# Normalising the softmax output: the sums copied to all rows of their head by one selector product, reciprocal and scaling from PSUM

## The chip, the cores and the metric

One core of a Trainium2 chip runs the kernel. It has five engines that work side by side, each with its own queue of instructions: TensorE (PE in the profile; its weight loads are PEld), VectorE (DVE), ScalarE (ACT), GpSimd (POOL) and SyncE (SP), which issues the DMA transfers. On-chip memory is SBUF, with 128 rows called partitions, and PSUM, into which TensorE writes its products; the kernel uses it in tiles of 512 float32 values a partition, called banks below. The metric is the device time of one launch in microseconds (us), as the median of several runs.

## The reference: what is computed

Two independent layers read inputs of length 2048 and width 448, and their outputs stand side by side. The first is a state-space convolution done by Fourier transforms. The second is attention over all keys with 16 heads of width 28, and the change lies there:

```python
scores = jnp.einsum("bhqd,bhkd->bhqk", q, k) * scale
p = _softmax(scores, axis=-1)
o = jnp.einsum("bhqk,bhkd->bhqd", p, v)
return (lambda x, *d: x.transpose(*d))(o, 0, 2, 1, 3).reshape(B, S, D) @ wo
```

The kernel computes exponentials first, multiplies them with the values, and divides the product by the sum of the exponentials at the end. That last division is what is changed.

## The kernel before

Attention is cut into 16 units: G = 4 groups of HG = 4 heads, times NQ = 4 blocks of CQ = 512 queries. Within a unit, NK = 16 steps go over blocks of 128 keys. One main loop of 256 steps runs through all of them. Each head has 32 partitions of a 128-partition tile: 28 value columns, then a column of ones (row DH = 28 of the head's 32), whose product with the exponentials is the softmax sum, and three columns of zeros.

A step issues its work in the order of the list ORDER (line 34): 'm' are products for the row maxima of a later unit (`max_mm`, tile pm), which VectorE reduces (ScalarE first copies the kdif one to tile rl); 's' are score products (`s_mm`, tile pss), which ScalarE turns into exponentials (tile p); 'v' is one of VectorE's power steps for the convolution kernel (tiles g and zg); 'pv' is the value product (`pv_step`, tile po); 'k' is other work on the convolution kernel; 'f' is a slot in which one job of the rest is done. From the main loop on, all engines keep the order in which the program is written (`KEPT["a"]`), so an instruction that waits holds up everything behind it on its engine.

What a slot does is decided in `slot` (line 957): first whatever stands in the list `urgent` and is due, then the output projection, the parts of the convolution kernel, the transform of the input, and the spectrum and finishing jobs. `soon_slot(gap, f)` (line 950) puts f into `urgent`, due `gap` slots later. The gaps are in UG (line 40).

Every max product and every job in a slot takes a PSUM bank from `w_tile` (line 125), and the banks go round in a ring: three in the main loop (pool ps_m, line 562), four once the convolution kernel is complete (pool ps_f, line 1016). A bank can be written again only when its last reader is done.

When a unit's last value product is issued, `fin` (line 734) copies it from PSUM to tile o by ScalarE and puts two parts into slots. `sums` (gap 2): 16 small products with o as the weights and the selector `sel` (128x4) as the moving operand turn the sums into a layout with queries on the partitions; VectorE takes the reciprocal of 16 values a partition (tile r), and ScalarE spreads them over 512 columns (tile rb). `scale` (gap 4): 16 products with the identity turn rb back to heads on the partitions, and VectorE multiplies with o into tile on. A float32 product shows as two records, so these are 32 records each. For the first three groups, on is stored to DRAM (`on_d`) for later; for the last group it goes into the output projection (`project`, with tile og for the stored groups and the weights in tile ua), four products of 128 queries that come due PD = 2 steps after `fin`. `mm32` splits a product into pieces of 32 weight columns that run at once in four column groups of TensorE.

Of the kernel before, what the change touches and what calls it, by code (L numbers as in the profile page):

```python
# [8 lines left out]
F32 = mybir.dt.float32  # L9
F32R = mybir.dt.float32r  # L10
I32 = mybir.dt.int32
AF = mybir.ActivationFunctionType
# [9 lines left out]
DH = 28  # L22
G = 4
HG = H // G
# [12 lines left out]
FX, PD, GAP = 1, 2, 3  # L37
FL = {"s": 2, "f": 3}
S0, SP, SW, SD, PW, E3 = 0, 4, 0, 5, 37, 8
UG = (2, 2, 4)  # L40
PS = 1
SGB, XB, XL = 2, 5, 4
K0, KP, KD, UP = 0, 3.5, 4, 3
# [47 lines left out]
def body(ctx, tc, a, out):  # L91
    nc = Engines(tc)
# [4 lines left out]
    def pool(stack, name, bufs=1, space=None, side=None):  # L97
        kw = {} if space is None else {"space": space}
        if side:
            kw["side"] = side  # L100
        return stack.enter_context(tc.tile_pool(name=name, bufs=bufs, reuse_waits="tile", **kw))
# [13 lines left out]
    const = pool(ctx, "const")  # L115
    ident = const.tile([128, 128], F32, name="ident")
    nc.sync.dma_start(ident, a["ident"])
    sel = const.tile([128, HG], F32, name="sel")
    kones = const.tile([128, 1], F32, name="kones")
    w1 = const.tile([128, 2, 128], F32, name="w1")  # L120

# [3 lines left out]
    def w_tile():  # L125

        n_ring[0] += 1
        return ps_w[0].tile([128, CQ], F32, name=f"pm{n_ring[0] % ps_w[1]}")
# [7 lines left out]
    def mm32(o, w, x_, start, stop, at=0):  # L136

        for i in range(w.shape[-1] // 32):
            c = slice(32 * i, 32 * i + 32)
            nc.tensor.matmul(o[c], w[:, c], x_, start=start, stop=stop, tile_position=(0, at + 32 * i))  # L140
# [53 lines left out]
    def max_join(u):  # L194
        m_u[u, 1] = q_p.tile([128, HG * 4], F32, name="m1", bufs=2)
        nc.vector.tensor_reduce(m_u[u, 1], m_u[u].rearrange("p a b c -> p (a b) c"), axis=AX.X, op=ALU.max)
# [15 lines left out]
    with ExitStack() as st:  # L212
# [47 lines left out]
        t = a["A_log_dt"]  # L260
# [294 lines left out]
    kq_p = pool(kq_st, "kq_p")  # L555
# [178 lines left out]
    def fin(u, s_):  # L734
        g, c = divmod(u, NQ)
        o = kq_p.tile([128, CQ], F32, name="o")
        nc.scalar.activation(o, o_u[u], AF.Copy)
        on = kq_p.tile([128, CQ], F32, name="on", bufs=2)
        rb = kq_p.tile([128, 4, HG, 32], F32, name="rb")
        og = og_u.pop(u, None)  # L740

        def sums():
            pw = w_tile()
            for t in range(4):
                mm32(pw[:, t * HG:(t + 1) * HG], o[:, t * 128:(t + 1) * 128], sel, start=True, stop=True)
            r = kq_p.tile([128, 4, HG], F32, name="r", bufs=2)
            nc.vector.reciprocal(r, pw[:, :4 * HG].rearrange("p (t h) -> p t h", h=HG))
            nc.scalar.activation(rb, r[:, :, :, None].to_broadcast([128, 4, HG, 32]), AF.Copy)

        def scale():  # L750
            pw = w_tile()
            for t in range(4):
                mm32(pw[:, t * 128:(t + 1) * 128], rb[:, t].rearrange("p h e -> p (h e)"), ident, True, True)
            nc.vector.tensor_tensor(on, o, pw, ALU.mult)
            if g < G - 1:
                nc.sync.dma_start(on_d[c][g], on)
            else:
                p_due.extend((s_ + PD + PS * t, lambda t=t: project(t)) for t in range(4))

        def project(t):  # L760
            pw = w_tile()
            ts = slice(t * 128, (t + 1) * 128)
            for g2 in range(G):
                mm32(pw[:, :D], og[:, g2, ts] if g2 < G - 1 else on[:, ts], wo_t[g2 // 2][:, g2 % 2, :],
                     start=g2 == 0, stop=g2 == G - 1)
            y = kq_p.tile([128, D], F32, name="y", bufs=2)
            nc.scalar.activation(y, pw[:, :D], AF.Copy)
            q0 = c * CQ + t * 128
            nc.sync.dma_start(out[q0:q0 + 128, D:], y)

        soon_slot(UG[1], sums)
        soon_slot(UG[2], scale)

    fk = {}

# [174 lines left out]
    def soon_slot(gap, f):  # L950
        n_urgent[0] += 1
        urgent.append((n_slot[0] + gap, n_urgent[0], f))
        q = sorted(urgent)
        urgent.clear()
        urgent.extend(q)
# [38 lines left out]
    def k_next():  # L994

        if last[0] is not None and not powers["e"] and not powers["g"]:
            if last[0] + 3 < NB:
                load_sd(last[0] + 3)
            last[0] = None
# [6 lines left out]
    for s in range(NS):  # L1006
# [26 lines left out]
        for op in ORDER:  # L1033
            if op[0] == "s":
                ps.append(s_mm(u, kt, int(op[1])))
            elif op[0] == "f":
                slot(s)
            elif op[0] == "v":
                vec()
            elif op == "k":  # L1040
                k_next()
                k_begin(s)
                k_seed(s)
                for _ in range(3):
                    if powers["e"]:
                        powers["e"].popleft()()
            elif op == "pv":
                if prev:
                    pv_step(*prev)
                    if prev[1] == NK - 1:  # L1050
                        fin(prev[0], s)
            elif sm < NS:
                max_mm(sm // NK, sm % NK, int(op[1]))
        for _ in range(FX if late[0] else 0):
            slot(s)
        if sm < NS and sm % NK == NK - 1:
# [3 lines left out]
            max_join(sm // NK)  # L1060
            soon_slot(UG[0], end)
        k_next()
        prev = (u, kt, ps)
    pv_step(*prev)
    fin(prev[0], NS)
    s = NS
    while urgent or p_due or m_due or u_due or any(q[k] for q in (f_jobs, f_tasks, f_loaded) for k in "sf"):
# [7 lines left out]
def constants():  # L1075
    import numpy as np
    k = {}
    k["ident"] = np.eye(128)
    sel, ones = np.zeros((128, HG)), np.zeros((128, 1))
    for j in range(HG):  # L1080
        sel[32 * j + DH, j] = 1.0
        ones[32 * j + DH:32 * j + DH + 2] = 1.0
    k["sel"], k["kones"] = sel, ones
    k["pw2"] = np.tile(2.0 ** np.arange(LV), (128, 1))
    n1, k1 = np.arange(N1), np.arange(N1)
    n2, k2 = np.arange(N2), np.arange(N2)
    th = 2 * np.pi * np.outer(n1, k1 + 0.25) / N1
    w1 = np.zeros((2, 128, 128))
    wb = np.zeros((2, 2, N1, 2, N1))
    for j in range(4):  # L1090
        w1[0, 32 * j:32 * j + 32, 32 * j:32 * j + 32] = np.cos(th)
        w1[1, 32 * j:32 * j + 32, 32 * j:32 * j + 32] = np.sin(th)
    for h in range(2):
        wb[h, 0, :, h, :] = np.cos(th).T / L
        wb[h, 1, :, h, :] = np.sin(th).T / L
    k["w1"] = w1.transpose(1, 0, 2)
    k["wb"] = wb.transpose(0, 1, 2, 4, 3).reshape(128, N2)
    ph = 2 * np.pi * ((k1[:, None, None] + 0.25) * n2[None, :, None] / L + n2[None, :, None] * k2[None, None, :] / N2)
    c, s = np.cos(ph).transpose(1, 0, 2), np.sin(ph).transpose(1, 0, 2)
    m2 = np.zeros((2, N2, N1, 2, 64))  # L1100
    m2[0, :, :, 0], m2[0, :, :, 1] = c, s
    m2[1, :, :, 0], m2[1, :, :, 1] = -s, c
    k["m2u"] = m2.reshape(2, 16, 4, N1, 128).transpose(1, 0, 2, 3, 4).reshape(128, N1, 128)
    wa = np.zeros((2, 64, N1, N2, 2))
    ct, st = c.transpose(2, 1, 0), s.transpose(2, 1, 0)
    wa[0, ..., 0], wa[0, ..., 1] = ct, -st
    wa[1, ..., 0], wa[1, ..., 1] = st, ct

    wa = wa.reshape(2, 64, N1, 2, 2, 16, 2).transpose(0, 1, 2, 5, 4, 3, 6)
    k["mw"] = np.concatenate([m2.reshape(128, N1, 128), wa.reshape(128, N1, 128)], -1)  # L1110
    return {n: v.astype(np.float32) for n, v in k.items()}
# [18 lines left out]
```

## Time and profile before

| | |
|---|---|
| median of 3 runs | 1304.37 us (1303.61 to 1306.14) |
| span of the profiled execution | 1301.1 us |
| the runs' median less this span | 3.3 us |
| normalisations in the span | 16; reciprocals from 320.0 to 1279.4 us |
| mean granted TensorE clock | 0.978 of full speed |

The profiled execution is one run of the program, read by the hardware's profiler; its span goes from the first to the last instruction. A row of a group of instructions gives the line, engine, operation, output<-input tiles, the shape, the count, then the busy time in us and the mean length of one in ns, then the idle time of the engine ahead of them with what ended it. All lines read L75, because a helper there records every operation; the tiles tell the operations apart. A row of a timeline gives the start and the length in us. A row of a table by stretches gives the stretch, its length, then busy time and instruction count of PE, PEld, DVE, ACT and POOL, the granted TensorE clock, the share of DMA time and GB/s. The ends of matmuls are modelled and consecutive ones overlap, so distances from start to start tell more than lengths.

### The profile page before, as it was taken

What the parts mean: (1) busy time and instruction counts of PE and PEld (TensorE: products, weight loads), DVE (VectorE), ACT (ScalarE), POOL (GpSimd) and SP (SyncE); (2) the same over time, 40 slices, a digit from 0 to 9 for tenths busy, and PEclk for the clock granted to TensorE, in tenths of its full rate; (3) what the DMA queues carried; (4) which work ended last, traced back from release to release, by engine and by line L of the source; (5) the groups of instructions that cost most, each with busy time, mean ns of one, the idle gap of its engine ahead of it and who ended that gap; (6) DMA issues with size and microseconds to landing.
All of it is one profiled execution on the core that took longest, in us unless ns stands there. A gap on an engine that the chain in (4) does not pass through costs nothing.

```text
span 1301.1 us, 33177 instructions
## 1 busy us (share of the span) xinstructions
PE 1228.2 (94%) x12625; PEld 701.0 (54%) x12625; DVE 948.0 (73%) x2106; ACT 952.4 (73%) x2068; POOL 871.1 (67%) x736
## 2 busy tenths in 40 slices
PE   6878985899999999999999999999999999999997
PEld 5657763355555555555555555555555555544433
DVE  5887896987777887787788888888888655645111
ACT  4775763488888888888888888888887766756552
POOL 3676683298888878888869999998996212424421
PEclk9888997999999999999999999999999999999999
DMA  6677769835866555458644131733425453647656
GB/s 194 203 258 244 249 206 294 237 77 124 195 137 149 124 146 148 140 147 231 181 126 96 54 95 32 182 91 83 103 51 148 153 158 133 201 144 244 198 162 174
DMA packets 200088, 205.35 MB, mean 158 GB/s; under 512 B 95993, under 2 KB 158521, under 8 KB 197881
## 3 DMA queue, kind: packets, MB, share of 16 engines
q1 hardware_dynamic: 199928, 203.23, 56.2%
q8 instruction: 100, 1.64, 0.5%
q14 instruction: 60, 0.48, 0.1%
HBM read 120.73 MB, written 82.18 MB: 156 GB/s over the span
## 4 chain that ended last, share of the span: by engine, by line
PE 71%; DVE 10%; DMA 6%; POOL 5%; ACT 3%; issue 3%; SPq 0%; POOLq 0%; ACTq 0%; DVEq 0%
PE pm L75 40%; PE pss L75 16%; PE po L75 15%; DVE tri L75 2%; DVE mx L75 2%; POOL e L75 1%; POOL qhat L75 1%; DMA k<-hl 1%; ACT tri L75 1%; DVE qhat L75 1%; DVE sg L75 1%; DMA tri<-in_B_wqkv 1%; DVE px L75 1%; DMA khat<-k 1%; DMA ut<-in_A_u 1%
## 5 line engine op out<-in xcount | busy, mean ns | idle before, releaser
L75 ACT ACTIVATE p<-pss 128x512 f32<-128x512 f32 x1024 | 560.9, 609 | 111.6 <-PE pss L75 108.6
L75 PE MATMUL pss<-qhat,khat 128*128 128x512 f32 x1024 | 402.5, 399 | 1.5 <-ACT p L75 1.4
L75 DVE TENSOR_REDUCE mx<-pm 128x1 f32<-128x512 f32 x500 | 321.4, 684 | 109.2 <-PE pm L75 107.1
L75 PE MATMUL pm<-khat,qhat 128*128 128x512 f32 x749 | 326.3, 438 | 3.4 <-DVE mx L75 2.1
L75 POOL TENSOR_TENSOR e<-e,sdb 128x256 f32<-128x256 f32 x168 | 202.0, 1202 | 116.2 <-ACT e L75 61.2
L75 PE MATMUL po<-p,v 128*32 128x512 f32 x2048 | 269.1, 594 | 0.0
L75 POOL TENSOR_TENSOR e<-e,eu 128x256 f32<-128x256 f32 x168 | 248.4, 1478 | 13.2
L75 PEld LDWEIGHTS pm<-khat,qhat 128*128 128x128 f32 x749 | 141.0, 189 | 199.7 <-ACT p L75 47.8
L75 DVE CUSTOM_DVE_ANT_0 rl<-pm,rl 128x512 f32<-128x512 f32 x249 | 171.4, 688 | 65.2 <-ACT rl L75 61.5
L75 PEld LDWEIGHTS pss<-qhat,khat 128*128 128x128 f32 x1024 | 190.2, 188 | 45.7 <-issue 10.8
L75 POOL TENSOR_TENSOR eu<-e,sdb 128x256 f32<-128x256 f32 x168 | 202.2, 1203 | 0.0
L75 POOL TENSOR_TENSOR p<-pr,pr 64x448 f32<-64x448 f32 x64 | 73.3, 1145 | 158.5 <-PE pm L75 133.2
L75 ACT ACTIVATE rl<-pm 128x512 f32<-128x512 f32 x249 | 150.8, 606 | 20.4 <-PE pm L75 20.4
L75 DVE TENSOR_TENSOR g<-g,zg 128x128 f32<-128x128 f32 x392 | 162.1, 413 | 3.4
L75 PE MATMUL pm<-xh,khat 112*128 112x512 f32 x256 | 94.1, 451 | 23.2 <-DVE hl L75 11.1
L75 PE MATMUL pm<-kdif,qhat 128*128 128x512 f32 x249 | 100.5, 404 | 2.6 <-DMA v<-v 1.3
L75 DVE TENSOR_TENSOR zg<-g,zg 128x128 f32<-128x128 f32 x224 | 88.0, 393 | 5.0
L75 PEld LDWEIGHTS pm<-e,g 128*32 128x32 f32 x3584 | 57.2, 109 | 43.8 <-issue 16.1
L75 DVE TENSOR_TENSOR pr<-pm,ub 128x448 f32<-128x448 f32 x64 | 37.0, 619 | 56.4 <-PE pm L75 42.0
L75 PEld LDWEIGHTS pm<-xh,khat 112*128 112x128 f32 x256 | 54.2, 217 | 39.4 <-DVE hl L75 12.9
L75 PE MATMUL pm<-e,g 128*32 128x64 f32 x3584 | 73.0, 222 | 1.9 <-POOL e L75 1.9
L75 ACT ACTIVATE y<-pm 128x448 f32<-128x448 f32 x48 | 26.5, 553 | 58.2 <-PE pm L75 33.8
(134 smaller groups left out, 1470.3 us busy)
## 6 DMA issues: line engine op xcount, KB each, us to landing
sdb<-sd SPq DMA_DIRECT2D x56, 336.0 KB
khat<-k SPq DMA_DIRECT2D x64, 256.0 KB
qhat<-q SPq DMA_DIRECT2D x64, 256.0 KB
sd<-sg SPq DMA_DIRECT2D x8, 1456.0 KB
k<-hl SPq DMA_DIRECT2D x16, 512.0 KB
q<-hl SPq DMA_DIRECT2D x16, 512.0 KB
mw<-in_mw SPq DMA_DIRECT2D x16, 512.0 KB
sd<-qhat SPq DMA_DIRECT2D x8, 896.0 KB
```

The lines of the kernel that those rows point to most:

```text
L75: i = f(*args, **kw)
```

## The change

The selector is now 128x128: column 32j to 32j+31 have their one in the row that holds the sum of head j. One product with this selector as the weights and o as the moving operand puts each head's sum on all 32 partitions of the head, for all 512 queries. VectorE takes the reciprocal of the whole 128x512 block in place in PSUM and multiplies it with o into on. The part `sums`, the tiles r and rb and ScalarE's copy are gone, and `scale` moves into the slot that `sums` had.

```diff
-UG = (2, 2, 4)
+UG = (2, 2)
...
-    sel = const.tile([128, HG], F32, name="sel")
+    sel = const.tile([128, 128], F32, name="sel")
...
         on = kq_p.tile([128, CQ], F32, name="on", bufs=2)
-        rb = kq_p.tile([128, 4, HG, 32], F32, name="rb")
         og = og_u.pop(u, None)
-
-        def sums():
-            pw = w_tile()
-            for t in range(4):
-                mm32(pw[:, t * HG:(t + 1) * HG], o[:, t * 128:(t + 1) * 128], sel, start=True, stop=True)
-            r = kq_p.tile([128, 4, HG], F32, name="r", bufs=2)
-            nc.vector.reciprocal(r, pw[:, :4 * HG].rearrange("p (t h) -> p t h", h=HG))
-            nc.scalar.activation(rb, r[:, :, :, None].to_broadcast([128, 4, HG, 32]), AF.Copy)
 
         def scale():
             pw = w_tile()
-            for t in range(4):
-                mm32(pw[:, t * 128:(t + 1) * 128], rb[:, t].rearrange("p h e -> p (h e)"), ident, True, True)
+            mm32(pw, sel, o, start=True, stop=True)
+            nc.vector.reciprocal(pw, pw)
             nc.vector.tensor_tensor(on, o, pw, ALU.mult)
...
-        soon_slot(UG[1], sums)
-        soon_slot(UG[2], scale)
+        soon_slot(UG[1], scale)
...
-    sel, ones = np.zeros((128, HG)), np.zeros((128, 1))
+    sel, ones = np.zeros((128, 128)), np.zeros((128, 1))
     for j in range(HG):
-        sel[32 * j + DH, j] = 1.0
+        sel[32 * j + DH, 32 * j:32 * j + 32] = 1.0
```

## The prediction

> **What bounds the kernel now.** I read the page first (busy time and the chain that ended last), then the same busy times by stage.
>
> ```profile
> span 1301.1 us, 33177 instructions
> PE 1228.2 (94%) x12625; PEld 701.0 (54%) x12625; DVE 948.0 (73%) x2106; ACT 952.4 (73%) x2068; POOL 871.1 (67%) x736
> ...
> PE 71%; DVE 10%; DMA 6%; POOL 5%; ACT 3%; issue 3%; SPq 0%; POOLq 0%; ACTq 0%; DVEq 0%
> ```
> ```profile
> 300.00:900.00 600.00, 595.93 (x7150) 331.60 (x7142) 489.69 (x1165) 503.27 (x1158) 514.04 (x404) 1.00 0.54 132
> 900.00:1050.00 150.00, 148.82 (x1719) 84.37 (x1715) 120.92 (x279) 118.84 (x259) 105.41 (x83) 1.00 0.41 114
> 1050.00:1200.00 150.00, 149.64 (x1496) 76.77 (x1488) 81.15 (x167) 93.79 (x184) 44.03 (x36) 1.00 0.55 172
> ```
> In the second fence the busy times stand in the order PE, PEld, DVE, ACT, POOL; then comes the granted clock. TensorE sets the end and is never without work from 300 us on. But VectorE is not far behind where most of the change falls: 490 of 600 us and 121 of 150 us, 81% busy. It has little idle time to take up new work before 1050 us and much after it.
>
> **What goes and what comes, by the groups of instructions.** Busy us, then the mean of one in ns:
>
> ```profile
> L75 PE MATMUL pm<-sel,o 128*32 128x4 f32 x512 | 7.0, 175 | 0.3 <-ACT o L75 0.3
> L75 PE MATMUL pm<-ident,rb 128*32 128x128 f32 x512 | 17.3, 275 | 0.7 <-ACT rb L75 0.7
> L75 ACT ACTIVATE rb<-r 128x512 f32<-128x512 f32 x16 | 10.1, 630 | 5.0 <-DVE r L75 5.0
> L75 DVE RECIPROCAL r<-pm 128x16 f32<-128x16 f32 x16 | 4.0, 250 | 0.0
> L75 DVE TENSOR_TENSOR on<-o,pm 128x512 f32<-128x512 f32 x16 | 10.9, 683 | 2.3 <-PE pm L75 2.1
> L75 DVE TENSOR_SCALAR mh<-pm 16x128 fp32r<-16x128 f32 x15 | 4.2, 277 | 5.9 <-PE pm L75 5.5
> L75 DVE TENSOR_SCALAR dt_all<-pt 56x8 f32<-56x8 f32 x5 | 0.5, 150 | 0.3 <-PE pt L75 0.3
> L75 DVE TENSOR_SCALAR px<-px 8x56 f32<-8x56 f32 x5 | 0.9, 177 | 0.1
> ```
> Sixteen times in the run (once per group of heads and block of queries) a unit is normalised. I give each part its price.
>
> *The reciprocal grows from 16 to 512 elements a row; no row shows one of that length.* VectorE's other operations that read PSUM fix the scale: 8 elements take 150 ns and 128 take 277, so (277-150)/120 = 1.06 ns an element and 150-8 = 142 ns beside. A reciprocal of 16 at that rate would take 159 ns; it took 250. The excess of 91 ns is either a fixed cost, or the reciprocal is slower for each element. The lower bound is the first: 250 + 496 x 1.06 = 0.78 us. If the fixed part is 142 ns, an element costs (250-142)/16 = 6.8 ns and 512 take 3.6 us. If the fixed part is the smaller one of the 8x56 row (177-56 x 1.06 = 118 ns), an element costs 8.3 ns and 512 take 4.35 us. The upper bound, no fixed part at all, is 250/16 x 512 = 8.0 us. I take 3.6: it uses the fixed part of operations that, like this one, read PSUM, and a fixed surplus of 91 ns for one opcode has no like among these rows. The Trainium skill says, in "VectorE: DVE Perf Modes", section "First, the fixed hardware budget", that the reciprocal runs as an iterative divide with a repeat count of 8. By it 512 elements would be an estimated 8 x 1.06 x 512 = 4.3 us, close to the 4.35 case; the row alone can't tell 6.8 from 8.3 ns.
>
> That the result goes back to PSUM I cost at nothing: the same power step writes SBUF in 412 ns and PSUM in 425.
>
> ```profile
> L75 DVE TENSOR_TENSOR g<-g,zg 128x256 f32<-128x256 f32 x224 | 92.4, 412 | 1.5
> L75 DVE TENSOR_TENSOR zg<-g,zg 128x256 f32<-128x256 f32 x168 | 71.4, 425 | 3.1
> ```
>
> *TensorE.* Two rounds of 32 records go; one of 8 records of 128x512 comes, the shape of a value product (po). I take one unit, the normalisation at 874 us, as the example, first TensorE, then VectorE (columns: start, length, engine):
>
> ```profile
> 874.16 0.43 PE L75 MATMUL pm<-sel,o 128*32 128x4 f32 x32
> 874.44 1.06 PE L75 MATMUL po<-p,v 128*32 128x512 f32 x8
> 875.43 0.50 PE L75 MATMUL pm<-khat,qhat 128*128 128x512 f32 x1
> ...
> 876.47 0.39 PE L75 MATMUL pm<-kdif,qhat 128*128 128x512 f32 x1
> ...
> 877.71 1.08 PE L75 MATMUL pm<-ident,rb 128*32 128x128 f32 x32
> 878.61 1.04 PE L75 MATMUL po<-p,v 128*32 128x512 f32 x8
> 879.47 0.63 PE L75 MATMUL pm<-e,g 128*32 128x64 f32 x32
> ```
> ```profile
> 875.62 0.25 DVE L75 RECIPROCAL r<-pm 128x16 f32<-128x16 f32 x1
> 875.79 0.38 DVE L75 TENSOR_TENSOR g<-g,zg 128x256 f32<-128x256 f32 x1
> 876.09 1.28 DVE L75 TENSOR_REDUCE mx<-pm 128x1 f32<-128x512 f32 x2
> ```
> From start to next start the sums hold TensorE 0.28 us (874.16 to 874.44) and the spreading product 0.90 (877.71 to 878.61); a product of po's shape 0.86 (878.61 to 879.47). So 1.18 goes and 0.86 comes: 0.3 us gained a unit.
>
> *ScalarE* loses a copy of 0.63 us. It is 84% busy at most (503 of 600) and not the bound: nothing on the path. *SP*: the selector's load grows from 2 to 64 KB, at 16 us, with its first use at 319; the store of the scaled output is now queued two slots earlier, ahead of the next query load, which is needed only a unit (some 57 us) later. The freed slot brings other due work forward but takes none away. All nothing.
>
> *The wait that comes.* In the main loop three PSUM banks go round among max products, jobs and this product, and every engine keeps program order. In the example the selector product takes one bank, the next two max products (the first at 875.43) the others, and the third (the kdif one, 876.47) needs the first bank again: it is free only when reciprocal and scaling are through. After the change: product 874.16 to 875.0, so the value product and all behind it come 0.6 later (0.86-0.28); the reciprocal starts as before at about 875.65, behind the work ahead of it on VectorE, ends at 879.25, the scaling (0.68) at 879.9. TensorE reaches the third product at 876.47+0.6 = 877.05 and stands until 879.9: 2.85 us. Queued behind on VectorE are the power step and the two maxima of 876.09; the second of the following products needs the bank of the first maximum (about 880.9) and loses another 0.5. The slot that held the spreading product thus comes 0.6+2.85+0.5 = 3.9 later, and saves 0.9: **+3.0 us**. Where VectorE has idle time right behind, the second wait drops out and +2.5 stays. I take the mean, 2.75, for the twelve units before 1050 us. If TensorE did not stand at all, the price would be the product's -0.3.
>
> *The clock after such a gap.* A standing TensorE is slowed in this trace. A gap of 1.66 us was followed by 3.4 us at half clock, while one of 1.27 us left the clock alone:
>
> ```profile
> 140.68 0.73 PE L75 MATMUL pm<-xh,khat 112*128 112x512 f32 x2 [1.66 <-DVE hl L75]
> 138.40:141.80 3.40, 1.74 (x11) 1.31 (x10) 3.37 (x9) 2.39 (x9) 3.40 (x4) 1.00 0.14 49
> 141.90:145.20 3.30, 3.30 (x9) 2.55 (x9) 3.30 (x4) 0.56 (x2) 3.22 (x3) 0.50 0.89 311
> 145.30:148.60 3.30, 3.02 (x19) 2.42 (x18) 3.30 (x3) 2.64 (x4) 2.76 (x4) 1.00 0.13 35
> 688.84 0.37 PE L75 MATMUL pm<-e,g 128*32 128x64 f32 x12 [1.27 <-POOL e L75]
> 688.80:692.20 3.40, 3.36 (x49) 1.89 (x49) 1.57 (x4) 1.50 (x6) 3.24 (x5) 1.00 0.38 135
> ```
> A stand of 2.85 us lies above both. Half clock over 3.4 us costs 1.7 us of TensorE work; some 0.4 of it hides under VectorE's remaining lag, and I let it happen in 85% of the units, since a gap may fall across two of the 3.4 us spells: 1.3 x 0.85 = 1.1 us. The bounds are 0 and 1.7. The Trainium skill ("TensorE: Matmul & The Clock Gate", section "Part 1: The HAM clock gate (the "warmup" mystery)") puts the return to half rate after an idle window of about 3.4 us. By that a stand of 2.85 us would be free of it and the sum 14.5 us lower, the rival below; here the 1.66 us gap was enough, so I go by the row.
>
> *The last four units.* At 1055 and 1131 us the ring has four banks and VectorE is 54% busy; the fourth turn is the kdif product:
>
> ```profile
> 1055.38 0.25 DVE L75 RECIPROCAL r<-pm 128x16 f32<-128x16 f32 x1
> ...
> 1057.44 0.40 PE L75 MATMUL pm<-kdif,qhat 128*128 128x512 f32 x1
> ```
> It comes at 1058.0 (0.6 later), and the bank is free at 1055.45+3.6+0.7 = 1059.75: a stand of 1.75, then some 0.7 for the two products whose banks VectorE still has to read, so 0.6+1.75+0.7-0.9 = 2.2, and a half clock in half of them (0.65). Near 1209 us there are no maxima any more and the ring lasts for three slots: no stand, -0.3. Near the end:
>
> ```profile
> 1281.57 0.69 DVE L75 TENSOR_TENSOR on<-o,pm 128x512 f32<-128x512 f32 x1 [1.46 <-PE pm L75]
> 1283.51 0.94 PE L75 MATMUL pm<-ua,on 128*32 128x448 f32 x8
> ```
> The scaled block, ready at 1282.3 now, is ready at about 1284.2: the selector product starts at 1278.8, then 0.9, a pause of 0.2, 3.6 and 0.7. Its first use at 1283.5 would come earlier by at most the 0.9 saved, and now waits: I take +0.5.
>
> **Sum.** 12 x (2.75+1.1) = 46.2; 2 x (2.2+0.65) = 5.7; -0.3 and +0.5: +52 us. On the span that is 1301.1+52 = 1353; the median of the runs, 1304.37, lies 3.3 above the span, which gives **1356 us**.
>
> **Rivals.**
> - *Slower still: 4.35 us a reciprocal.* 0.75 more in 14 units, 10.5 us: 1367. For it: the 118 ns fixed part. Against: that row reads SBUF.
> - *Stands without the half clock.* 12 x 1.1 + 2 x 0.65 = 14.5 less: 1342. For it: the clock is 1.00 in every stage row from 300 to 1200 us, and the dips lie in the sparser first stage. Against: the 1.66 us gap.
> - *The wait is mostly hidden.* VectorE idles 19%, so 2.2 us of the 12 us after each unit; if all of it took up the 3.35 us added, 1.15-0.3 = 0.85 would stay, times 14: 1316. Against: the ring stops TensorE 1.4 us after the reciprocal's start, long before that idle time comes round.
> - *Not slower: the reciprocal runs at an element each 1.06 ns and 0.78 us holds.* Its place is the bank's third turn. That comes 1.4 us after the reciprocal's start (875.65 to 877.05) and the scaling needs 0.68, so up to a reciprocal of 0.7 us nobody waits. At 0.78 the gain of 0.3 in 16 units remains, with a little from the lost turn: 1298. For it: nothing in the trace forbids a fixed surplus. Against: it would be the only one.
>
> **How the numbers follow.** Forecast 0.42; 4.35 us 0.20; no half clock 0.17; mostly hidden 0.08; not slower 0.10; a reciprocal near 8 us, 1304+52+4.4 x 14 = 1418, 0.03. The range 1324 to 1377 takes the first three with 10 to 18 us on either side, for how many units fall into half clock, and leaves out the other three. A measurement here tells about 0.2% (2.6 us) from no change. Faster 0.08 and the same 0.02 come from the case "not slower", with 0.01 each for what I have not thought of: 0.09, 0.03, and slower 0.88.
>
> **What would show it.** The reciprocal's row at 3.6 us (0.78 and 4.35 are the other cases). After each of the first twelve a TensorE gap of 2 to 3 us in front of a pm product, put down to VectorE, and in most of them 3.4 us at 0.50. ScalarE 10 us less busy, VectorE about 54 us more (16 x 3.35), TensorE's records of sel and rb replaced by 128 of about 590 ns. I am wrong if the reciprocal is near 1 us, or if TensorE goes on past it.

## The result, and the profile after

The changed kernel takes 1357.18 us (median of 4 runs, 1356.38 to 1362.36) against 1303.99 us before (4 runs): a ratio of 1.0413, with a 95% interval of 1.0392 to 1.0433. The forecast was 1356 us. The profiled execution takes 1354.3 us, 53.2 more than before.

The page of the changed kernel first:

```profile
span 1354.3 us, 31395 instructions
...
PE 1240.5 (92%) x11729; PEld 691.3 (51%) x11729; DVE 999.4 (74%) x2106; ACT 946.2 (70%) x2052; POOL 871.1 (64%) x736
...
PE 68%; DVE 16%; ACT 5%; POOL 4%; issue 3%; DMA 3%; SPq 0%; ACTq 0%; POOLq 0%; DVEq 0%
```
VectorE's busy time grew by 51 us and its share of the chain that ended last from 10% to 16%. TensorE executes 896 records fewer and yet needs longer. The groups that answer to those of before:

```profile
L75 DVE RECIPROCAL pm<-pm 128x512 f32<-128x512 f32 x16 | 53.8, 3361 | 2.4 <-PE pm L75 2.3
L75 DVE TENSOR_TENSOR on<-o,pm 128x512 f32<-128x512 f32 x16 | 11.0, 688 | 0.7
L75 PE MATMUL pm<-o,sel 128*32 128x512 f32 x128 | 17.0, 605 | 0.3 <-ACT o L75 0.3
L75 PE MATMUL pm<-khat,qhat 128*128 128x512 f32 x749 | 329.7, 443 | 31.4 <-DVE on L75 26.7 <-DVE mx L75 2.0 <-ACT rl L75 1.3
```
The last of these groups before the change:

```profile
L75 PE MATMUL pm<-khat,qhat 128*128 128x512 f32 x749 | 326.3, 438 | 3.4 <-DVE mx L75 2.1
```
A reciprocal takes 3.36 us, and the max products, which had 3.4 us of idle time ahead of them before, now have 31.4, most of it ended by VectorE's scaling (on). One normalisation shows how; TensorE, then VectorE, then three stretches with the clock in the third column from the right:

```profile
843.43 1.06 PE L75 MATMUL pm<-o,sel 128*32 128x512 f32 x8
844.31 1.04 PE L75 MATMUL po<-p,v 128*32 128x512 f32 x8
845.17 0.63 PE L75 MATMUL pm<-e,g 128*32 128x64 f32 x32
845.73 0.50 PE L75 MATMUL pm<-khat,qhat 128*128 128x512 f32 x1
846.07 0.40 PE L75 MATMUL pss<-qhat,khat 128*128 128x512 f32 x1
849.14 0.47 PE L75 MATMUL pm<-khat,qhat 128*128 128x512 f32 x1 [2.67 <-DVE on L75]
849.45 0.59 PE L75 MATMUL pss<-qhat,khat 128*128 128x512 f32 x1
```
```profile
844.91 3.36 DVE L75 RECIPROCAL pm<-pm 128x512 f32<-128x512 f32 x1
848.30 0.69 DVE L75 TENSOR_TENSOR on<-o,pm 128x512 f32<-128x512 f32 x1
848.91 0.42 DVE L75 TENSOR_TENSOR zg<-g,zg 128x256 f32<-128x256 f32 x1
849.24 1.28 DVE L75 TENSOR_REDUCE mx<-pm 128x1 f32<-128x512 f32 x2
```
```profile
846.60:849.30 2.70, 0.16 (x1) 0.19 (x2) 2.67 (x4) 0.56 (x1) 2.54 (x4) 1.00 0.01 6
849.50:852.80 3.30, 3.30 (x26) 2.23 (x28) 2.65 (x7) 2.17 (x4) 3.14 (x4) 0.50 0.86 240
852.90:856.20 3.30, 3.30 (x20) 1.58 (x16) 2.02 (x5) 2.37 (x6) 3.22 (x3) 1.00 1.14 213
```
The selector product takes bank one, the job (e,g) bank two, the first max product bank three, and the second max product needs bank one. It waits 2.67 us until the scaling is through, and the 3.4 us that follow run at half clock.

To see where the 53.2 us lie, I take from each trace the start of the first value product of every unit, and from these the length of the units. A normalisation falls into the unit after its own. Differences to before, in us:

| stretch | before, us | changed | slot kept (e1) | copy (e2) | copy, slot kept (e3) | stands filled (e7) |
|---|---|---|---|---|---|---|
| start, before any normalisation | 318.9 | +2.0 | +1.4 | -0.5 | +1.8 | -0.9 |
| normalisations 1 to 11 | 669.3 | +37.3 | +38.7 | -1.9 | -2.2 | +26.8 |
| normalisation 12 | 66.5 | +11.7 | +3.8 | +11.5 | -0.3 | +2.3 |
| normalisations 13 and 14 | 155.9 | +5.2 | +4.6 | +1.7 | -0.6 | +3.3 |
| the last two, to the end | 90.5 | -3.0 | +1.0 | -4.5 | -1.7 | +0.8 |

The first eleven units of the changed kernel are longer by 2.2, 2.6, 3.7, 4.2, 2.4, 2.2, 4.0, 3.9, 3.8, 4.2 and 4.0 us. They fall into two groups, and the granted clock tells them apart: the four below 3 us have no spell at half clock behind the stand, the seven above have one of 3.4 us. So the stand costs 2.4 us a unit, and a half clock 1.6.

The twelfth unit is the surprise: +11.7 us. Here TensorE stands for 6.46 us, 15 us after the normalisation, and for another reason. GpSimd's queue after, and the same work before:

```profile
1025.74 1.31 POOL L75 TENSOR_TENSOR e<-e,eu 128x512 f32<-128x512 f32 x1
1042.28 4.77 POOL L75 TENSOR_TENSOR p<-pr,pr 64x448 f32<-64x448 f32 x4 [15.23 <-DVE pr L75]
1047.12 1.91 POOL L75 TENSOR_TENSOR e<-e,sdb 128x1024 f32<-128x1024 f32 x1
1048.99 1.91 POOL L75 TENSOR_TENSOR eu<-e,sdb 128x1024 f32<-128x1024 f32 x1
1050.98 2.32 POOL L75 TENSOR_TENSOR e<-e,eu 128x1024 f32<-128x1024 f32 x1
...
1053.35 1.08 PE L75 MATMUL pm<-e,g 128*32 128x64 f32 x32 [6.46 <-POOL e L75]
```
```profile
992.26 2.39 POOL L75 TENSOR_TENSOR e<-e,eu 128x1024 f32<-128x1024 f32 x1
1003.53 4.81 POOL L75 TENSOR_TENSOR p<-pr,pr 64x448 f32<-64x448 f32 x4 [8.88 <-PE pm L75]
```
Before, the last power step (its last operation is the one at 992.26) came ahead of the first joins of the spectrum job (p<-pr). Now the joins come first. They need products that TensorE issues late, so GpSimd waits 15.23 us for them with the three operations of the last power step queued behind, and the last (e,g) products wait for these. The job came earlier because the change freed a slot. A stretch at half clock follows here too:

```profile
1050.90:1057.60 6.70, 4.25 (x57) 1.88 (x57) 0.00 (x0) 0.22 (x1) 2.32 (x2) 0.50 0.00 0
```

### The profile page after: what moved, and what is told of

Same layout as the page of the kernel before. It is cut to its first block, busy times and chain, and to the rows that moved or that the text cites. A ratio compares the mean times of both kernels' runs of the same rounds, so it can differ in the third digit from the quotient of the medians.

```text
span 1354.3 us, 31395 instructions
## 1 busy us (share of the span) xinstructions
PE 1240.5 (92%) x11729; PEld 691.3 (51%) x11729; DVE 999.4 (74%) x2106; ACT 946.2 (70%) x2052; POOL 871.1 (64%) x736
## 4 chain that ended last, share of the span: by engine, by line
PE 68%; DVE 16%; ACT 5%; POOL 4%; issue 3%; DMA 3%; SPq 0%; ACTq 0%; POOLq 0%; DVEq 0%
PE pm L75 38%; PE pss L75 15%; PE po L75 14%; DVE pm L75 3%; DVE mx L75 3%; DVE tri L75 2%; DVE rl L75 2%; ACT p L75 1%; POOL qhat L75 1%; ACT rl L75 1%; DVE qhat L75 1%; ACT tri L75 1%; POOL p L75 1%; DVE sg L75 1%; DVE px L75 1%
## 5 line engine op out<-in xcount | busy, mean ns | idle before, releaser
L75 PE MATMUL pm<-khat,qhat 128*128 128x512 f32 x749 | 329.7, 443 | 31.4 <-DVE on L75 26.7
L75 PE MATMUL po<-p,v 128*32 128x512 f32 x2048 | 272.2, 601 | 0.0
L75 PE MATMUL pm<-xh,khat 112*128 112x512 f32 x256 | 91.5, 440 | 22.5 <-DVE hl L75 11.7
L75 PEld LDWEIGHTS po<-p,v 128*32 128x32 f32 x2048 | 56.2, 111 | 34.3 <-issue 29.6
```

The costliest lines, as they stand in the source:

```text
L75: i = f(*args, **kw)
```

## The experiments

**e1, the freed slot kept empty.** Is the twelfth unit's loss one of the queue's order?

```diff
         soon_slot(UG[1], scale)
+        soon_slot(4, lambda: None)
```


> The changed kernel, with the slot that the change frees kept empty, so that all other jobs come in the order of before. Theory of the queue order: the gap of 6.46 us after the twelfth normalisation comes from GpSimd's queue, where the freed slot pulled the spectrum's joins ahead of the last power steps; with the slot kept that gap and the 6.8 us at half clock behind it are gone, and the time falls by 8 to 11 us to 1346 to 1349 us. Rival, the gap is another effect of the long reciprocal: the time stays at 1355 to 1359 us and the gap stays.

1353.96 us (1349.81 to 1358.01), ratio 1.0382 (1.0353 to 1.0412). The gap of 6.46 us is gone and the twelfth unit falls from +11.7 to +3.8, as the theory of the queue's order says; the rival has fallen. Yet the medians fell by 3 us and not by 8 to 11, and the runs' ranges overlap. In the profiles the twelfth unit gives 7.9 back and the end takes 4.0, where the freed slots had let the last jobs finish sooner. The next two runs show the same without the stands.

**e2 and e3, a copy in place of the reciprocal,** without and with the slot kept; the division is left out.

```diff
-            nc.vector.reciprocal(pw, pw)
+            nc.vector.tensor_copy(pw, pw)
```


> The changed kernel with the reciprocal of 128x512 replaced by a copy of the same block in place in PSUM (the division is left out). Theory of the long reciprocal: the copy takes about 0.68 us, the stands of 2.3 to 2.9 us are gone and only the freed slot's loss of 8 to 11 us stays, against a gain of 0.3 us in 16 units: 1305 to 1311 us. Rival, the loss comes from the product's place, the earlier slot or the ring of banks and not from the length of the reciprocal: above 1335 us.

> The copy in place of the reciprocal (the division is left out) and the freed slot kept empty. Theory: neither loss is left and the gain of TensorE shows, 16 x 0.3 us with a little from the lost bank turn: 1295 to 1300 us, faster than before. Rival, the selector product itself costs more than it saves: 1304 us or more.

1308.0 us (ratio 1.0030, 1.0017 to 1.0042) and 1299.45 us (0.9964, 0.9951 to 0.9978). Both as the theory of the long reciprocal has it. The copy's row of the run with the slot kept:

```profile
L75 DVE COPY pm<-pm 128x512 f32<-128x512 f32 x16 | 11.1, 695 | 1.4 <-PE pm L75 0.8 <-ACT p L75 0.5
```
With 0.70 us where the reciprocal has 3.36, not one stand is left behind a normalisation, and everything else in the change is a small gain. The freed slot alone turns that gain of 0.4% into a loss of 0.3%, by the twelfth unit: +11.5 without and -0.3 with it.

**e4, the reciprocal in SBUF,** with the bank free as soon as ScalarE has copied it.

```diff
-            nc.vector.reciprocal(pw, pw)
-            nc.vector.tensor_tensor(on, o, pw, ALU.mult)
+            rs = kq_p.tile([128, CQ], F32, name="rs")
+            nc.scalar.activation(rs, pw, AF.Copy)
+            nc.vector.reciprocal(rs, rs)
+            nc.vector.tensor_tensor(on, o, rs, ALU.mult)
...
+        soon_slot(4, lambda: None)
```


> The freed slot kept empty; ScalarE copies the spread sums from PSUM to SBUF (0.6 us), and the reciprocal and the scaling read SBUF, so that the bank is free 2.7 us earlier. Theory of the held bank alone: TensorE no longer stands at the bank's third turn and the time falls to 1308 to 1320 us. Theory of VectorE's queue: the maxima behind the reciprocal come as late as before, TensorE stands at the bank of one of them instead, one or two products later, and the time stays within 5 us of the run with the slot kept, 1342 to 1351 us.

1382.59 us, ratio 1.0601 (1.0579 to 1.0624): worse than either theory said. VectorE at one normalisation, then TensorE's wait there, then all scalings (min/median/max in ns):

```profile
865.11 3.35 DVE L75 RECIPROCAL rs<-rs 128x512 f32<-128x512 f32 x1 [0.32 <-ACT rs L75]
...
868.50 1.47 DVE L75 TENSOR_TENSOR on<-o,rs 128x512 f32<-128x512 f32 x1
...
870.22 1.28 DVE L75 TENSOR_REDUCE mx<-pm 128x1 f32<-128x512 f32 x2
870.95 0.50 PE L75 MATMUL pm<-khat,qhat 128*128 128x512 f32 x1 [3.78 <-DVE mx L75]
```
```profile
L75 DVE TENSOR_TENSOR on<-o,rs x16: 691/1652/2721, 320.9 to 1356.6; 128x512 f32<-128x512 f32 x16
```
The held bank alone is not what costs. With the bank free, TensorE goes on for two max products more and stands at the third, whose bank still holds a product that VectorE has to reduce, and that maximum is queued behind the reciprocal: "<-DVE mx" in place of "<-DVE on". That is the theory of VectorE's queue. Two things can be seen that made it worse than that theory's 1342 to 1351 (no run takes them apart): ScalarE's copy sets the reciprocal back, and the scaling, both of whose operands now lie in SBUF, takes a median of 1.65 us against 0.69. The stands grow to 3.1 to 5.6 us in the first twelve, and eight of these have 6.8 us at half clock behind them.

**e7, the stand filled with work.** The max product behind the selector product is issued seven times more, into its own bank and with the same result.

```diff
+            fill[0] = 7
...
-            nc.tensor.matmul(pm, q, kt[:, kc * CQ:(kc + 1) * CQ], start=True, stop=True)
+            for _ in range(1 + fill[0]):
+                nc.tensor.matmul(pm, q, kt[:, kc * CQ:(kc + 1) * CQ], start=True, stop=True)
+            fill[0] = 0
```


> The run with the slot kept, and the max product that follows the selector product is issued seven times more into its own bank, to the same result: 7 x 0.23 = 1.6 us of TensorE work that fills the first part of the stand, so that some 1.1 us of it stay. Theory of the half clock: spells at half clock behind a normalisation cost about 1.6 us each (units with one run 3.8 to 4.6 us over before, units without 2.1 to 2.6), the profile of the run with the slot kept has ten of them after 400 us, and without them the time is 1336 to 1342 us, with no half clock after 260 us. Rival, the half clock hides under VectorE's lag: 1350 to 1358 us, as with the slot kept.

1335.76 us (1335.33 to 1340.14), ratio 1.0262 (1.0240 to 1.0283), just under the lower end of the expectation and 18 us under the run with the slot kept, with more work on TensorE:

```profile
836.99 2.11 PE L75 MATMUL pm<-khat,qhat 128*128 128x512 f32 x8
838.93 0.39 PE L75 MATMUL pss<-qhat,khat 128*128 128x512 f32 x1
840.39 0.47 PE L75 MATMUL pm<-khat,qhat 128*128 128x512 f32 x1 [1.07 <-DVE on L75]
```
Idle time is down to 1.07 us, the max product waits to the same moment of VectorE's scaling, and the clock stays at full from 254 us to the end of the work at 1330. The units are then 2.44 us over before, on average over the eleven (26.8/11; 2.1 to 2.8 each). So the stand and the half clock are two prices, and the second is a third of the whole loss.

**e9, the same with the slot given back in the last group.**

```diff
-        soon_slot(4, lambda: None)
+        if g < G - 1:
+            soon_slot(4, lambda: None)
```


> The run with the filled stands, with the freed slot kept for the first three groups alone and given to other jobs for the last one. Theory: the slot does harm at the twelfth unit only (GpSimd's joins ahead of the last power steps) and helps behind it, by some 3 us in the last two units (in the copy runs 65.1 against 67.0 us and 20.9 against 21.8 us): 1331 to 1334 us. Rival, the freed slots of the last group are worth nothing: 1335 to 1338 us.

1332.40 us, ratio 1.0218 (1.0205 to 1.0231): 3.4 us less, as expected, and in the profiles the last two units go from +0.8 to -3.0. With e1, the freed slot harms at one place and helps at another.

**e5, the reciprocal in four pieces,** at the places of VectorE's power steps, with the scaling on GpSimd.

```diff
+            def part(i):
+                cs = slice(128 * i, 128 * i + 128)
+                nc.vector.reciprocal(rs[:, cs], rs[:, cs])
+                if i == 3:
+                    nc.gpsimd.tensor_tensor(on, o, rs, ALU.mult)
...
     def vec():
+        if parts:
+            parts.popleft()()
```


> ScalarE copies the spread sums to SBUF, VectorE takes the reciprocal in four pieces of 128 columns, each at one of the next places of its power steps, GpSimd scales; the freed slot is kept for the first three groups. Theory that VectorE's one long instruction makes the loss, not its work as such: a piece takes about 0.95 us, no stand is longer than 1.3 us, the clock stays at full, and of 3.8 us added to VectorE a unit most goes into its idle time: 1300 to 1325 us. Rival, VectorE's added work counts in full where it is 81% busy: 12 x 3.5 us and more, 1340 us or above.

1351.18 us, ratio 1.0372 (1.0352 to 1.0391). The time is the rival's, but the run doesn't decide between the two, since a new wait came in (the group of the pieces, then GpSimd and TensorE at one normalisation):

```profile
L75 DVE RECIPROCAL rs<-rs 128x128 f32<-128x128 f32 x64 | 59.4, 939 | 9.7 <-ACT rs L75 9.7
```
```profile
849.23 1.27 POOL L75 TENSOR_TENSOR on<-o,rs 128x512 f32<-128x512 f32 x1 [7.50 <-DVE rs L75]
856.70 0.85 PE L75 MATMUL pm<-e,g 128*32 128x64 f32 x32 [2.88 <-POOL e L75]
```
GpSimd waits 7.50 us for the last piece and its power steps wait behind, and then TensorE for these. What the run gives is a price: a piece of 128 takes 0.94 us.

**e6, the reciprocal on ScalarE** as exp(-ln(sum)).

```diff
-            nc.vector.reciprocal(pw, pw)
+            nc.scalar.activation(rs, pw, AF.Ln)
+            nc.scalar.activation(pw, rs, AF.Exp, scale=-1.0)
```


> The reciprocal is taken by ScalarE as exp(-ln(sum)), from PSUM over SBUF back to PSUM, so that VectorE keeps only the scaling; the freed slot is kept for the first three groups. If no function table has to be loaded for it, ScalarE has 0.6 us a unit more than before, VectorE 0.25 us less, no stand comes, and the gain of TensorE and of the freed slots at the end shows: 1294 to 1301 us. If the tables are switched, two loads of 1.28 us a unit stand in ScalarE's queue ahead of the exponentials: 1305 to 1330 us.

1363.19 us, ratio 1.0460 (1.0438 to 1.0482): far above both.

```profile
791.86 1.28 ACT L75 ACT_TABLE_LOAD   x1
793.16 0.60 ACT L75 ACTIVATE rs<-pm 128x512 f32<-128x512 f32 x1
793.77 1.28 ACT L75 ACT_TABLE_LOAD   x1
795.07 0.60 ACT L75 ACTIVATE pm<-rs 128x512 f32<-128x512 f32 x1
```
The tables are switched twice a unit, and 3.8 us in one piece on ScalarE hold the bank and the exponentials as the long reciprocal held VectorE: the stands in the first twelve are 2.9 to 3.0 us. VectorE, in program order, stands 3.8 us at the scaling as well. I had priced the loads but not the stand. The Trainium skill ("ScalarE: Activation LUTs", section "Table sets: the hidden batching unit") names a set that holds exp and ln together, so that one load would do; this program got two.

**e10, before without ScalarE's spreading copy.** The products with the identity read the 16 reciprocals as weights, each repeated 32 times.

```diff
-                mm32(pw[:, t * 128:(t + 1) * 128], rb[:, t].rearrange("p h e -> p (h e)"), ident, True, True)
+                for i in range(HG):
+                    nc.tensor.matmul(pw[32 * i:32 * i + 32, t * 128:(t + 1) * 128], rr[0][:, t, i:i + 1].to_broadcast([128, 32]), ident,
+                                     start=True, stop=True, tile_position=(0, 32 * i))
```


> The kernel before, with ScalarE's spreading copy left away: the products with the identity read the 16 reciprocals with each repeated over 32 columns as their weights. Theory that this copy of 0.63 us lies beside the path: no change, 1301 to 1305 us. Rival, it delays the exponentials behind it on ScalarE: 16 x 0.3 to 0.6 us less, 1294 to 1299 us.

1300.50 us, ratio 0.9975 (0.9965 to 0.9985): a quarter of a per cent faster, a little more than the "no change" expected. Of the 3.2 us between the two profiles 1.1 lie ahead of the first normalisation, so the copy was nearly free.

**e11, the selector product with a short reciprocal.** The four sum rows go by DMA into 128x16, and the reciprocals back over the sum rows. In the first eleven units the two parts come due after 4 and 6 slots, two later than in the kernel before; from the twelfth on after 2 and 4.

```diff
+            for j in range(HG):
+                nc.sync.dma_start(rd[32 * j:32 * j + 32, :], row(j))
...
+        def turn():
+            nc.vector.reciprocal(rd, rd)
+            for j in range(HG):
+                nc.sync.dma_start(row(j), rd[32 * j:32 * j + 32, :])
...
+        elif u >= 11:
+            soon_slot(2, turn)
+            soon_slot(4, scale)
+        else:
+            soon_slot(4, turn)
+            soon_slot(6, scale)
```


> The selector product is kept, but the reciprocal is taken of 16 elements a row: the four sum rows of o go by DMA into a 128x16 tile, VectorE takes the reciprocal there (0.25 us), and DMAs write it back over the sum rows ahead of the selector product; the scaling reads the spread reciprocals from PSUM. Both slots are taken as before; the last unit keeps the long reciprocal. Theory that the length of the reciprocal is the whole loss: no stand, no half clock, TensorE's gain of 0.3 us a unit as in the copy run with the slot kept, 1297 to 1303 us. Rival, VectorE and the product wait for the DMAs, about 1 us or more a unit: 1310 us or above.

1423.78 us, ratio 1.0905 (1.0889 to 1.0921): the rival, and much more of it.

```profile
765.12 2.44 SPq L75 DMA_DIRECT2D o<-rd  x4
772.39 1.94 PE L75 MATMUL pm<-o,sel 128*32 128x512 f32 x8 [5.53 <-DMA o<-rd]
```
Issued at 765.12 behind the query loads, the write-back is there at 772.4. TensorE waits 95.3 us in all for such landings, in fifteen units, and the half clock comes on top.

**e12, the same with the waits taken away.** For the first eleven units the turn by DMA, with six slots for the way there and fourteen for the way back; for the last five the form of e10.

```diff
+        if by_dma:
+            soon_slot(6, turn)
+            soon_slot(20, spread)
+        else:
+            soon_slot(UG[1], sums)
+            soon_slot(UG[2], scale)
```


> For the first eleven units the reciprocal of 16 elements a row by way of the DMAs, with six slots (some 12 us) for the way there and fourteen (some 28 us) for the way back, then the selector product with scaling only; for the last five the kernel before without the spreading copy. Theory: what lost the time in the run by DMA was the wait for landings of 5 to 12.5 us and nothing else, so it goes, and TensorE gains 0.3 us in eleven units on top of the run without the copy: 1295 to 1300 us. Rival, the two lots of small DMAs or the moved slots cost as much as the product saves: 1301 to 1308 us.

1297.32 us (1295.45 to 1299.65), ratio 0.9951 (0.9934 to 0.9968). This beats both kernels, with the idea of the change, one selector product in place of two rounds, and a reciprocal of 16 elements:

```profile
L75 DVE RECIPROCAL rd<-rd 128x16 f32<-128x16 f32 x11 | 2.7, 246 | 0.0
```
The gain over e10 is small: the two ratios' intervals just overlap. In the profiles it lies where the selector product is: normalisations 1 to 11 take 5.6 us less than before, in e10 1.4 us less.

## Why the prediction was right, and where only in sum

*The reciprocal's price.* Taken 3.6 us, measured 3.36; the bounds were 0.78 and 8.0. From 16 to 512 elements it is (3361-250)/496 = 6.27 ns an element and some 150 ns beside; the piece of 128 fits (0.15+128 x 6.27 = 0.95, measured 0.94). So the excess of 91 ns in the short row was a rate and not a fixed cost, as argued, and the 8.3 ns case is too high. So is the estimate of 4.3 us after the Trainium skill ("VectorE: DVE Perf Modes", section "First, the fixed hardware budget"), with its repeat count of 8. "Not slower" fell with this, and by e2 and e3 the reciprocal's length decides: the same kernel with 0.70 us in its place shows none of the stands.

*The wait that comes.* The place was right, the bank's third turn. The size was 2.4 us a unit where I took 2.75: the second wait of 0.5 us in the example is not there (behind the twelve stands TensorE waits for a maximum once, 0.14 us). That it is the held bank is only half of it: e4 frees the bank, and the maxima queued behind on VectorE take its place.

*The clock.* Right, and shown by e7. The price was 1.6 us where I took 1.3, and it came in 7 of the first 11 units where I took 85%. By the Trainium skill's rule ("TensorE: Matmul & The Clock Gate", section "Part 1: The HAM clock gate (the "warmup" mystery)") an idle window of about 3.4 us would be needed. Here stands of 2.5 to 2.8 us were enough in seven of eleven, at full clock before; the rival without the half clock (1342) would have been too low by 15 us. Which stands it hits isn't settled by their length but by where they fall. In all thirteen traces the spells at half clock begin on a grid of 3.413 us (here at 849.48, 910.92 and 972.36, 18 steps apart each). The stand of 2.67 us at 846 us lies whole in one step, the one of 2.67 us at 390 us is divided between two:

```profile
846.07:849.48 3.41, 0.73 (x4) 0.33 (x3) 3.38 (x4) 0.93 (x3) 3.00 (x5) 1.00 0.03 10
849.49:852.89 3.40, 3.40 (x26) 2.24 (x28) 2.75 (x7) 2.25 (x5) 3.24 (x4) 0.50 0.87 240
388.68:392.09 3.41, 1.99 (x46) 0.89 (x34) 3.41 (x4) 1.42 (x4) 2.71 (x4) 1.00 0.62 153
392.10:395.50 3.40, 2.16 (x26) 1.62 (x30) 3.22 (x7) 1.42 (x3) 3.24 (x4) 1.00 0.57 179
395.51:398.90 3.39, 3.39 (x28) 1.68 (x16) 2.70 (x7) 2.87 (x8) 3.31 (x3) 1.00 1.08 222
```
In the traces from 255 us on, a step at full clock in which TensorE idled 1.9 us or more was always followed by half clock, one with less than 1.5 us never, and between these it went both ways. In e1 the first eleven stands are as long as here to 0.02 us, and yet other normalisations have half clock behind them (3 and 5 to 10 there, 3, 4 and 7 to 11 here). So the reason given for 85%, that a gap may fall across two spells, was right, and the share itself hangs on how the grid lies in a run.

*The freed slot.* This is the step that failed: "The freed slot brings other due work forward but takes none away. All nothing." It moved the joins ahead of the last power step in GpSimd's queue and cost 9 us at the twelfth normalisation (11.7 less 2.4 for the stand), and gave some 3 us back at the end. I had looked at SP's queue for what is moved and not at GpSimd's.

*The sum.* Forecast +52, profile +53.2, but partly by luck. Stands and half clock in the first twelve: 46.2 forecast, 37.3 in eleven and 2.4 in the twelfth, 39.7. The freed slot: nothing forecast, +9.3. Normalisations 13 and 14: 5.7 forecast, 5.2. The end: +0.2 forecast, -3.0. And 2.0 came before any normalisation, where of the change only the larger selector load acts; the profiles of the other runs differ from before there by -2.4 to +2.4, so this is no effect that they show.

## What to carry to other kernels

Price an operation by its rate for this opcode: two lengths of any other opcode tell the fixed part, and what a short instance takes beyond it is the rate to multiply (here that gave 3.6 us for a measured 3.36). A long instruction on an engine that is "only" 81% busy stops the engine that sets the time as soon as a ring of a few buffers has gone round, and freeing the buffer doesn't help when the readers of the other buffers are queued behind that instruction. When an edit frees or moves a slot in a planned order, look through the queue of every engine for what now stands in front of what; and an idle gap can cost a second time, by the clock, if most of it falls into one step of the clock's grid.

## What the hardware showed that I had not expected

- A scaling with both operands in SBUF took 0.69 us when GpSimd was idle and 1.47 to 2.72 us in all cases but one beside GpSimd's work (e4; the median of all sixteen is 1.65); with one operand in PSUM it took 0.68 to 0.69 each time. The Trainium skill ("GPSIMD Engine Reference", section "1. Specifications") says that GpSimd shares its SBUF interfaces with VectorE and contends with instructions that have two SBUF inputs; the runs agree.
- Seven extra products a unit that compute nothing new made a kernel 18 us faster, because they kept the clock up (e7 against e1).
- Four small DMAs of 2 KB each, issued behind larger loads, had all landed only some 7 us after the first of them was issued (e11).
